# Attention and MLP gradients on one core: dw1 stored from SyncE's ring behind the last V load, and the 15-engine dV stores moved to heads 8, 17 and 26

## Chip, cores and metric

The kernel runs on one core of one Trainium2 chip. The metric is the device time of one execution in microseconds (us). The kernel before took 405.26 us when the prediction was made (median of 3 runs, 404.29 to 406.43).

Five instruction engines appear: TensorE (PE), VectorE (DVE), ScalarE (ACT), GpSimd (POOL) and SyncE (SP). The transfers are done by 16 DMA engines. "Ring" is used for the queue of transfers that one instruction engine has issued: here SyncE's ring (all large loads and some stores) and GpSimd's ring (most stores). A transfer is cut into packets, the pieces that the trace records. A semaphore is a counter that an engine can wait for; a transfer has landed when its last increment has arrived.

## The reference

One token x of width 640 passes an attention branch and an MLP branch, mixed by a gate. The reference returns the output and the gradients with respect to x, both caches and all weights.

```python
q = (x @ wq).reshape(B, Sq, H, Dh)                         # H = 32 heads, Dh = 128
scores = einsum("bhqd,bhkd->bhqk", q, k_cache) * Dh**-0.5  # 4096 keys a head
p = softmax(scores);  a = einsum("bhqk,bhkd->bhqd", p, v_cache) @ wo
act = h * tanh(softplus(h));  b = act @ w2                 # h = x @ w1 + b1, F = 1728
out = g * a + (1 - g) * b                                  # g = sigmoid(sum(x * gate_w))
return (out, *vjp(grad_out))   # dx, dk_cache, dv_cache, dwq, dwo, dw1, db1, dw2, dgate_w
```

What matters is the traffic. K and V are 1 MB for each head and each cache, read once, and dK and dV are as large and are written once. With the weights and their gradients 82.03 MB are read and 82.03 MB written. dw1 is an outer product of 640 x 1728 in bf16, 2160 KB.

## The kernel before

The main loop goes through the heads; loads are issued three heads ahead by SyncE, stores of dV and dK by GpSimd except for the last two heads. Cuts are marked.

```python
def ring(h):
    return nc.sync if h >= H - 2 else nc.gpsimd
def load_v(h):
    if h < H:
        vts[h] = kv_in.tile([P, J, Dh], BF16, name="Vn", tag="Vn", bufs=VB)
        nc.sync.dma_start(vts[h][:], Vv[h])
# ... (load_k is alike)
def dwo():                                   # gradient of wo, one group of four heads
    # ...
    (nc.sync if g == NG - 1 else nc.gpsimd).dma_start(dwo_v[g], wos[g][:])
# ...
def dw1_part(rc):
    def f():
        nc.vector.tensor_scalar(w1_sb[:, rc, :], m["dh_bc"][:], x_f[:, rc:rc + 1], None, ALU.mult)
        if rc == RC - 1:
            nc.gpsimd.dma_start(dw1_v, w1_sb[:])
    return f
# ...
def dv_half(h, half):
    # ...
    if half == 1:
        if h % 10 == 9:
            spread(h // 10, dVv[h], st["dV"])
        else:
            ring(h).dma_start(dVv[h], st["dV"][:])

def spread(i, dst, t):                       # a "15-engine store"
    # ...
    if i == 0:
        nc.gpsimd.inc_swdge_sem([], [], mode="reset_dge_cursor")
    for a, b in (((120, 125), (0, 120), (125, 128)), ((0, 14), (14, 119), (119, 128)), ((0, 8), (8, 128)))[i]:
        nc.gpsimd.dma_start(out[a:b, :], src[a:b, :], max_dma_last_dim=J * Dh)
# ...
for h in range(H):
    # ...
    load_k(h + 3)
    load_v(h + 3)
    # ...
    period(h)                                # the dK and dV halves of earlier heads are made in here
# ...
dk_half(H - 1, 0)
dk_half(H - 1, 1)
# ...
for rc in range(RC):
    nc.vector.tensor_scalar(dwq_l[:, rc, :], dq_bc[:, CL:], x_f[:, rc:rc + 1], None, ALU.mult)
nc.sync.dma_start(dwq_v[:, :, CL:], dwq_l[:])
```

An ordinary dV store sends 128 rows of 8 KB, eight to each DMA engine. `spread` cuts the same 128 rows into two or three pieces whose largest has 120 or 105 rows. It is there to give one DMA engine less to do: the largest piece goes to 15 engines and leaves one out.

## Time and profile before

| | before |
|---|---|
| time, median of 6 runs (3 more were made beside the changed kernel) | 404.82 us (404.18 to 406.43) |
| span of the profiled run | 402.6 us |
| bytes moved | 164.93 MB, mean 410 GB/s |
| PE, DVE, ACT, POOL busy | 75%, 75%, 44%, 12% |
| last DVE instruction ends | 392.62 us |
| slowest DMA engine ends its last store | 401.49 us |

From the page of the kernel before, the span, the rate in 40 slices of 10.1 us and the sum of the transfers:

```profile
span 402.6 us, 13606 instructions
...
GB/s 290 420 413 408 422 424 418 419 426 421 423 424 419 395 421 414 421 425 423 423 419 425 425 423 416 412 425 423 421 425 422 424 420 424 424 415 367 413 396 216
DMA packets 27816, 164.93 MB, mean 410 GB/s; under 512 B 3164, under 2 KB 3868, under 8 KB 11884
```

No compute engine is near full, while the rate stays at 412 to 426 GB/s in most slices. The kernel is bound by its transfers. The rate is low at the start, at slice 37 (362 to 372 us) and in the last slice. The windows view of the kernel before shows these stretches; after the bounds and the length come busy time and number of instructions of PE, PEld, DVE, ACT and POOL, the granted TensorE clock, the busy share of the 16 DMA engines, and GB/s:

```profile
core 0: us, PE busy (x) PEld busy (x) DVE busy (x) ACT busy (x) POOL busy (x), PEclk, DMA share, GB/s
357.00:362.00 5.00, 2.72 (x40) 2.38 (x37) 1.34 (x3) 1.66 (x3) 0.89 (x1) 1.00 1.01 413
362.00:367.00 5.00, 2.25 (x50) 2.02 (x50) 4.12 (x8) 1.11 (x3) 1.75 (x2) 0.78 0.89 365
367.00:372.00 5.00, 4.28 (x75) 3.92 (x75) 4.10 (x7) 2.32 (x5) 0.00 (x0) 0.88 1.02 362
387.00:392.00 5.00, 0.45 (x1) 0.18 (x1) 4.72 (x21) 0.00 (x0) 0.00 (x0) 0.50 0.93 384
392.00:397.00 5.00, 0.28 (x1) 0.09 (x1) 0.55 (x3) 0.26 (x1) 0.00 (x0) 0.50 0.91 355
397.00:403.00 6.00, 0.00 (x0) 0.00 (x0) 0.00 (x0) 0.00 (x0) 0.00 (x0) 0.50 0.27 101
```

DVE has only 1.34 us of work between 357 and 362 us. The chain of waits of the kernel before, in the window from 320 us (start, us, what), says why:

```profile
332.40 0.67 POOL out_dram L631
333.25 0.89 POOL out_dram L546
334.14 2.64 issue
336.80 25.24 DMA out_dram<-dV_sb
362.13 1.23 DVE dK_sb L614
```

L546 is the dw1 store, issued by GpSimd. Behind it in the same ring the store of dV27 took 25.24 us, and the DVE instruction that makes dK29 had to wait for that store's buffer. The timeline of DVE shows the hole as a number in brackets, 3.79 us of waiting; its last line below is DVE's last instruction:

```profile
358.17 0.17 DVE L673 TENSOR_REDUCE m<-sA 128x1 f32<-128x32 f32 x1
362.13 1.23 DVE L614 TENSOR_TENSOR dK_sb<-ds_bf,qd 128x2048 bf16<-128x2048 bf16 x1 [3.79 <-DMA out_dram<-dV_sb]
...
392.44 0.18 DVE L823 CAST fin_bf<-fin 128x15 bf16<-128x15 f32 x1
```

The waits of SyncE's queue (total us, times, longest), for its last two stores, dwo7 (L375) and dwq_l (L791):

```profile
SPq L375 <- DMA out_dram<-dV_sb: 4.9, 1, 4.9
...
SPq L791 <- DMA out_dram<-dwq_t: 1.8, 1, 1.8
```

Both wait for an earlier store to land and not for DVE. The trace's semaphore records give the reason: dwo7 and dwq_l count their completion on the semaphore of an earlier store. dV31's store is done on its slowest DMA engine at 391.35 us, and dwo7 on the same semaphore is issued at 391.42 us.

Those records also have a view that the page lacks. Each of these transfers adds 16 to its semaphore, one by one; I read every increment as one DMA engine that has done its share. They are listed here as us after the first increment, for the last half of dK31 of the kernel before (first at 390.69 us):

```
before: 0.0 0.3 0.3 0.6 1.5 1.6 3.8 4.1 5.0 5.4 5.5 5.7 7.1 7.4 7.6 7.7
```

So the DMA engines are far apart: 7.7 us between first and last, with four within 0.6 us of the last. For the last V load the spread was 16.7 us (350.17 to 366.91), one engine 5.2 us behind the next.

### The profile page before, as it was taken

The numbers are of one execution on the slowest core, as the hardware profiler recorded it, in microseconds if no ns is written. First come the engines' busy times: TensorE is split into PE (matmuls) and PEld (weight loads), VectorE is DVE, ScalarE is ACT, GpSimd is POOL, SyncE is SP. The second block draws the span as 40 slices with busy tenths as digits, with TensorE's granted clock in tenths as the row PEclk, the third lists the DMA queues.
The fourth block names the chain that finished last, engine by engine and source line by source line (L and its number), as shares of the span: only waits on it lengthen the run. The fifth ranks groups of instructions, "written<-read, shape, count | busy, mean of one in ns | idle before, by whom it ended". The sixth has DMA issues, their size and how long they took to land.

```text
span 402.6 us, 13606 instructions
## 1 busy us (share of the span) xinstructions
PE 300.7 (75%) x5872; PEld 271.9 (68%) x5872; DVE 303.7 (75%) x791; ACT 177.6 (44%) x411; POOL 46.5 (12%) x93
## 2 busy tenths in 40 slices
PE   0688888678888788878876988739887888966510
PEld 0577888568877778778866878628776778856500
DVE  3339666646599999977669799855999996968980
ACT  1355455325453555546523556505554555533300
POOL 0001111010011311111101113101111112121000
PEclk9999999857999999989988899957999999998755
DMA  8999999999999999999999999999999999999995
GB/s 290 420 413 408 422 424 418 419 426 421 423 424 419 395 421 414 421 425 423 423 419 425 425 423 416 412 425 423 421 425 422 424 420 424 424 415 367 413 396 216
DMA packets 27816, 164.93 MB, mean 410 GB/s; under 512 B 3164, under 2 KB 3868, under 8 KB 11884
## 3 DMA queue, kind: packets, MB, share of 16 engines
q1 hardware_dynamic: 16480, 91.20, 54.9%
q0 software_dynamic: 11216, 72.85, 43.7%
q8 instruction: 46, 0.75, 0.7%
q14 instruction: 14, 0.11, 0.1%
q10 hardware_dynamic: 60, 0.01, 0.0%
HBM read 82.03 MB, written 82.03 MB: 407 GB/s over the span
## 4 chain that ended last, share of the span: by engine, by line
DMA 35%; DVE 35%; PE 19%; ACT 4%; issue 3%; POOL 0%; ACTq 0%; SPq 0%; POOLq 0%; DVEq 0%
DMA Kn<-in_A_k_cache_dram 28%; DVE dK_sb L614 9%; PE tr L589 8%; DVE dV_sb L614 7%; DMA out_dram<-dV_sb 6%; DVE junk L385 4%; ACT tT L591 3%; PE sA L669 3%; DVE junk L288 3%; PE sA L598 2%; PE sB L722 2%; DVE junk L537 2%; DVE junk L494 1%; DMA vec_rows<-in_gate_w_dram 1%; DVE dj L709 1%
## 5 line engine op out<-in xcount | busy, mean ns | idle before, releaser
L591 ACT COPY tT<-tr 128x512 f32<-128x512 f32 x256 | 142.6, 588 | 138.9 <-PE tr L589 138.0
L598 PEld LDWEIGHTS <-tT 128*128 128x128 bf16 x2048 | 80.0, 98 | 43.9 <-ACT tT L591 33.8
L589 PE MATMUL tr<-ident_f,Kn 128*128 128x128 f32 x512 | 82.8, 300 | 12.8 <-DMA Kn<-in_A_k_cache_dram 12.8
L614 DVE TENSOR_TENSOR dK_sb<-ds_bf,qd 128x2048 bf16<-128x2048 bf16 x64 | 77.8, 1216 | 4.1 <-DMA out_dram<-dV_sb 3.8
L614 DVE TENSOR_TENSOR dV_sb<-p_bf,qd 128x2048 bf16<-128x2048 bf16 x64 | 78.0, 1218 | 0.6 <-DMA out_dram<-dK_sb 0.4
L589 PE MATMUL tr<-ident_f,Vn 128*128 128x128 f32 x512 | 74.3, 281 | 0.0
L589 PEld LDWEIGHTS tr<-ident_f,Kn 128*128 128x128 f32 x512 | 61.9, 153 | 14.2 <-issue 14.2
L598 PE MATMUL sA<-qd,tT 128*128 128x48 bf16 x1024 | 48.9, 187 | 23.4 <-ACT dq_all L727 12.7
L589 PEld LDWEIGHTS tr<-ident_f,Vn 128*128 128x128 f32 x512 | 57.3, 144 | 0.0
L598 PE MATMUL sB<-qd,tT 128*128 128x48 bf16 x1024 | 46.2, 183 | 0.0
L669 PEld LDWEIGHTS <-Vn 128*128 128x128 bf16 x1024 | 30.6, 96 | 10.6 <-issue 10.6
L669 PE MATMUL sA<-e_bf,Vn 128*128 128x48 bf16 x1024 | 31.2, 184 | 7.8 <-DVE zs L689 6.3
L631 POOL DMA_DIRECT2D out_dram<-dK_sb x30 | 17.2, 574 | 149.0 <-DVE rz L691 102.2
L722 PE MATMUL sB<-ds_bf,Kn 128*128 128x48 bf16 x1024 | 32.9, 187 | 1.4 <-DVE ds_bf L711 1.4
L673 DVE TENSOR_REDUCE m<-sA 128x1 f32<-128x32 f32 x32 | 6.0, 189 | 35.8 <-PE sA L598 29.1
L722 PEld LDWEIGHTS <-Kn 128*128 128x128 bf16 x1024 | 30.3, 99 | 1.6 <-issue 1.6
L644 POOL DMA_DIRECT2D out_dram<-dV_sb x27 | 14.6, 540 | 136.7 <-DVE o_all L714 48.1
L288 DVE SCALAR_TENSOR_TENSOR junk<-wo_g,da_bc 128x640 bf16<-128x640 bf16 x32 | 26.2, 820 | 1.7 <-ACT da_bc L229 1.1
L385 DVE SCALAR_TENSOR_TENSOR junk<-wq_g,dq_bc 128x1024 bf16<-128x1024 bf16 (+1 forms) x25 | 25.1, 1004 | 0.2
L693 ACT ACTIVATE p_bf<-e_bf,rz 128x64 bf16<-128x64 bf16 x32 | 11.1, 348 | 13.6 <-DVE rz L691 10.8
L700 DVE SCALAR_TENSOR_TENSOR pj<-sB,e_bf 128x32 f32<-128x32 f32 x32 | 6.1, 190 | 13.1 <-PE sB L598 12.9
L709 DVE TENSOR_SCALAR_CACHE_REDUCE dj<-sB,rz 128x128 f32<-128x128 f32 x32 | 11.1, 346 | 6.4 <-PE sB L703 6.4
(153 smaller groups left out, 275.4 us busy)
## 6 DMA issues: line engine op xcount, KB each, us to landing
Kn<-in_A_k_cache_dram SPq DMA_DIRECT2D x32, 1024.0 KB, 24.3
Vn<-in_A_v_cache_dram SPq DMA_DIRECT2D x32, 1024.0 KB, 28.8
out_dram<-dK_sb POOLq DMA_DIRECT2D x30, 1024.0 KB, 12.0
out_dram<-dV_sb POOLq DMA_DIRECT2D x27, 1024.0 KB, 11.3
wq_g<-in_A_wq_dram SPq DMA_DIRECT2D x4, 1280.0 KB, 19.7
wo_g<-in_A_wo_dram SPq DMA_DIRECT2D x8, 640.0 KB, 14.9
out_dram<-wo_g POOLq DMA_DIRECT2D x7, 640.0 KB, 11.6
out_dram<-dwq_t SPq DMA_DIRECT2D x4, 896.0 KB, 14.5
```

The lines of the kernel that those rows point to most:

```text
L288: nc.vector.scalar_tensor_tensor(junk[:, 0:D], in0=wos[g][:, i, :], scalar=1.0, in1=da_bc[:], op0=ALU.mult, op1=ALU.mult, accum_out=gp["do ...
L385: nc.vector.scalar_tensor_tensor(junk[:, c0:c1], in0=wqs[w][:, rc, c0:c1], scalar=1.0, in1=dq_bc[:, w * WG * Dh + c0:w * WG * Dh + c1], op ...
L589: nc.tensor.transpose(tp[:, t, :], flat[:, k * P:(k + 1) * P], ident_f[:])
L591: nc.scalar.copy(sb[:].rearrange("p a b -> p (a b)"), tp[:].rearrange("p a b -> p (a b)"))
L598: nc.tensor.matmul(out[:, 2 * k:2 * k + W], lhsT=tb[:, t, par, :], rhs=vec[:, par, :].unsqueeze(1).to_broadcast([P, W // 2, 2]), start=(pa ...
L614: nc.vector.tensor_tensor(dst[:, a:b, :].rearrange("p j (a b) -> p j a b", b=2), col[:, a:b, :].unsqueeze(2).to_broadcast([P, n, Dh // 2, 2]),
L631: ring(h).dma_start(dKv[h], st["dK"][:])
L644: ring(h).dma_start(dVv[h], st["dV"][:])
L669: nc.tensor.matmul(O, lhsT=vts[h][:, j, :], rhs=st["e"][:, j:j + 1].to_broadcast([P, W]), start=(j == 0), stop=(j == J - 1))
L693: nc.scalar.activation(p_bf[:], e[:].unsqueeze(2).to_broadcast([P, J, 2]), ACT.Copy, scale=rz[:])
L709: nc.vector.tensor_scalar(dj[:], PT, rz[:], None, ALU.mult, ALU.add, accum_out=dd[:])
L722: nc.tensor.matmul(DQ, lhsT=kts[h][:, j, :], rhs=ds[:, j, 0:1].to_broadcast([P, W]), start=(j == 0), stop=(j == J - 1))
```

## The change

The intent: the 2160 KB of dw1 stand in GpSimd's ring ahead of stores whose buffers DVE needs back. Put behind the last V load in SyncE's ring, where nothing follows that anybody waits for soon, dw1 delays nothing. The third 15-engine store comes at head 29 before, when the last loads have been issued; at head 26 it can still bring them forward.

```diff
             def f():
                 nc.vector.tensor_scalar(w1_sb[:, rc, :], m["dh_bc"][:], x_f[:, rc:rc + 1], None, ALU.mult)
-                if rc == RC - 1:
-                    nc.gpsimd.dma_start(dw1_v, w1_sb[:])
             return f
@@ dv_half
         if half == 1:
-            if h % 10 == 9:
-                spread(h // 10, dVv[h], st["dV"])
+            if h in (8, 17, 26):
+                spread(h // 9, dVv[h], st["dV"])
@@ main loop
+    stored = []
     for h in range(H):
         # ...
         load_k(h + 3)
         load_v(h + 3)
+        if h + 3 == H - 1 and f"dw1_{RC - 1}" in done:
+            nc.sync.dma_start(dw1_v, w1_sb[:])
+            stored.append(1)
@@ after the loop
-    assert len(dwqt) == RC
+    assert len(dwqt) == RC and stored
```

## The prediction

> **What bounds the kernel now.** The transfers. The page: 164.93 MB in 402.6 us. The windows view gives a DMA share of 1.01 to 1.02 and 413 to 425 GB/s for every 5 us from 322 to 362 us. Losses are at the start (290 GB/s in slice 1), at 362 to 372 us (365 and 362 GB/s) and in the last 6 us (share 0.27).
>
> The DMA engines are not equally far. By the sixteen completion increments of single transfers in the trace, the last K load (issued at 337.0) was done on its first engine at 345.4 and on its last at 361.8; the last V load at 350.2 and 366.9, with the slowest engine 5.2 us behind the next. At the end the spread is still 7.7 us (last dK half: 390.7 to 398.4), with four engines within 0.6 us of the last. The slow engines always have loads queued (load latency 20 to 38 us), so I read them as never idle: the kernel ends when they have moved their bytes.
>
> **What the change does.**
> 1. The dw1 store (2160 KB; at 420 GB/s 5.2 us of all engines) leaves GpSimd's ring at 333.25 us and stands in SyncE's ring behind the last V load, at about 337.9. No bytes are saved. The Trainium skill ("DMA: Bandwidth & Descriptors", Queues, rings and completion order) says that an engine goes round-robin between the rings it has work for. The trace agrees: dw1 took 23.7 us to land, and the dV and dK stores behind it 25.2, 25.6 and 23.5 us, where those before took 10 to 13. So the store of dV27 (issued 336.8) should land near 350 and not at 362.0, and the 3.79 us wait of DVE before dK29 (end of the 25.24 us link of the chain), and 0.37 us after it, go.
> 2. The third 15-engine store moves from head 29 (355 us) to head 26 (327 us), before the last loads. It spares the slowest engine 64 KB, 8 packets of about 310 ns, 2.5 us. With both, I expect the last K and V loads 3 to 6 us earlier. The other two move by one and two heads, which matters nowhere.
>
> DVE's instructions stay; their chain should end about 4 us earlier (388 to 389 instead of 392.6).
>
> **How much counts.** Little. Every engine moves the same bytes in both kernels, with three 15-engine stores either way, and those that end the kernel were busy throughout. Ending DVE's chain earlier only queues the last stores earlier: dwo7 and dwq_l already waited 4.9 and 1.8 us for earlier stores to land (waits of SyncE's queue), not for DVE. What fills is the dip at 362 to 372 us, idle time of the engines that are ahead. Against it: more of the tail is stores alone, where 8 KB packets took 315 to 336 ns. Sum: 0 to 1 us gained.
>
> **Predicted: 404.6 us, 402.4 to 406.6.** Faster by over 2%: 0.02; within: 0.96; slower: 0.02.
>
> **What would show it.** Right: no DVE wait on the dV store near 358 us; stores issued from 336 to 356 land in 10 to 15 us; the last V load lands at 361 to 364; no dip at 362 to 372; last DVE instruction near 389; and yet a spread of 6 to 9 us on the last stores, and the span within 1.5 us. Wrong: that spread falls below 5 us, or the span shrinks by the 4 us of the DVE chain.
>
> **What would make it wrong.** If the slow engines had idle time in the tail that I don't see, up to 4 us (1%) come. If the 15-engine stores relieve another engine at the new places, the end spread grows and 1 to 2 us are lost.

## The result, and the profile after

Ratios here and below are the mean time of one kernel's fast runs over that of the other's of the same rounds, so not quite the ratio of the medians that are quoted.

| | before | after |
|---|---|---|
| median of 6 runs | 404.82 us (404.18 to 406.43) | 404.14 us (403.89 to 404.53) |
| ratio to before (95% interval) | | 0.998 (0.9961 to 0.9999) |
| span of the profiled run | 402.6 us | 402.3 us |
| last DVE instruction ends | 392.62 us | 388.21 us |
| last V load done on its last engine | 366.91 us | 360.47 us |
| dV27's store, issue to landing | 25.2 us | 16.7 us |
| dw1's store, issue to landing | 23.7 us | 37.7 us |
| dwo7 and dwq_l issued | 391.42, 393.60 us | 391.31, 393.48 us |
| slowest DMA engine ends its last store | 401.49 us | 401.22 us |

All the local effects came: the DVE wait went, the loads came earlier, DVE ended 4.4 us earlier. The kernel's end moved by 0.3 us in the profiled runs.

The page of the kernel after (slice 37 is full now, slices 39 and 40 have less):

```profile
span 402.3 us, 13607 instructions
...
GB/s 283 418 416 406 419 424 420 418 422 424 422 422 418 423 414 403 425 423 423 422 421 424 423 422 419 418 426 425 421 423 425 421 424 417 425 420 417 424 368 189
```

The windows of the kernel after, same columns:

```profile
357.00:362.00 5.00, 3.72 (x68) 3.26 (x67) 4.96 (x11) 3.06 (x8) 1.14 (x2) 1.00 1.02 422
362.00:367.00 5.00, 4.47 (x104) 4.02 (x100) 4.96 (x10) 1.94 (x5) 1.50 (x2) 1.00 1.01 417
367.00:372.00 5.00, 4.28 (x92) 3.96 (x90) 4.04 (x9) 3.17 (x8) 0.00 (x0) 1.00 1.02 420
387.00:392.00 5.00, 0.27 (x1) 0.09 (x1) 1.11 (x5) 0.26 (x1) 0.00 (x0) 0.50 0.76 315
392.00:397.00 5.00, 0.00 (x0) 0.00 (x0) 0.00 (x0) 0.00 (x0) 0.00 (x0) 0.50 0.88 344
397.00:403.00 6.00, 0.00 (x0) 0.00 (x0) 0.00 (x0) 0.00 (x0) 0.00 (x0) 0.50 0.13 47
```

The dip is gone: (417 - 365) and (420 - 362) GB/s over 5 us each are 0.55 MB moved earlier. They are missing at the end: (384 - 315) + (355 - 344) over 5 us and (101 - 47) over 6 us are 0.72 MB. The bytes that filled the dip came from the share of DMA engines that would have finished early anyhow; they now idle at the end.

The timeline of DVE of the kernel after, without a bracket at dK29 and with an earlier end:

```profile
358.81 0.18 DVE L671 TENSOR_REDUCE m<-sA 128x1 f32<-128x32 f32 x1
358.91 1.22 DVE L612 TENSOR_TENSOR dK_sb<-ds_bf,qd 128x2048 bf16<-128x2048 bf16 x1
...
388.03 0.18 DVE L825 CAST fin_bf<-fin 128x15 bf16<-128x15 f32 x1
```

The waits of SyncE's queue of the kernel after:

```profile
SPq L375 <- DMA out_dram<-dV_sb: 8.9, 1, 8.9
...
SPq L793 <- DMA out_dram<-dwq_t: 1.8, 1, 1.8
```

The wait for dwo7 grew by 4.0 us, nearly all that DVE gained. Read alone, this suggests a rival reason for the small result: DVE's gain was real, and SyncE's wait for a landing swallowed it. The increments of the last half of dK31 suggest another (first at 388.50 us after, 390.69 us before):

```
before: 0.0 0.3 0.3 0.6 1.5 1.6 3.8 4.1 5.0 5.4 5.5 5.7 7.1 7.4 7.6 7.7
after:  0.0 0.3 0.3 0.5 0.6 1.3 4.1 5.4 5.6 6.3 6.8 6.9 7.0 7.1 7.2 9.6
```

In absolute time the second-last engine moved from 398.25 to 395.68 us, but the last only from 398.44 to 398.09. Before, four engines ended together; after, one stands alone, 2.4 us behind. The last increments of the last five stores come at 395.63, 396.85, 398.09, 399.64 and 401.22 us, 1.2 to 1.6 us apart for shares of 32 to 40 KB. I read them as this one engine working back to back; it ends the kernel. The recorded packets bear this out. They carry start, length and queue but no engine; yet they can be chained, as a packet mostly starts 3 or 4 ns before the end of the one before it, and the sizes must come in the order of the transfers. In the kernel after, the chain of the last engine goes back from 400.9 to 366.2 us, 201 packets with no pause over 1 ns. This is a reconstruction, which no view shows.

### The profile page after: what moved, and what is told of

Its sections match the earlier page's. It is cut to its first block, busy times and chain, and to the rows that moved or that the text cites. A ratio compares the mean times of both kernels' runs of the same rounds, so it can differ in the third digit from the quotient of the medians.

```text
span 402.3 us, 13607 instructions
## 1 busy us (share of the span) xinstructions
PE 298.5 (74%) x5872; PEld 270.1 (67%) x5872; DVE 303.1 (75%) x791; ACT 177.4 (44%) x411; POOL 45.6 (11%) x92
## 4 chain that ended last, share of the span: by engine, by line
DVE 40%; DMA 27%; PE 20%; issue 5%; ACT 4%; POOL 0%; ACTq 0%; SPq 0%; POOLq 0%
DMA Kn<-in_A_k_cache_dram 22%; DVE dK_sb L612 10%; DVE dV_sb L612 9%; PE tr L587 8%; DVE junk L385 5%; DMA out_dram<-wo_g 4%; ACT tT L589 4%; PE sA L667 3%; DVE junk L288 3%; PE sA L596 3%; PE sB L720 2%; DVE junk L537 2%; DVE junk L494 1%; DMA vec_rows<-in_gate_w_dram 1%; DVE wo_g L374 1%
## 5 line engine op out<-in xcount | busy, mean ns | idle before, releaser
L587 PE MATMUL tr<-ident_f,Kn 128*128 128x128 f32 x512 | 81.9, 298 | 12.6 <-DMA Kn<-in_A_k_cache_dram 12.6
L587 PEld LDWEIGHTS tr<-ident_f,Kn 128*128 128x128 f32 x512 | 61.2, 152 | 13.9 <-issue 13.9
## 6 DMA issues: line engine op xcount, KB each, us to landing
Kn<-in_A_k_cache_dram SPq DMA_DIRECT2D x32, 1024.0 KB, 23.7
```

The costliest lines, as they stand in the source:

```text
L587: nc.tensor.transpose(tp[:, t, :], flat[:, k * P:(k + 1) * P], ident_f[:])
```

## The experiments

The theories:

- A: the kernel ends when one DMA engine, which never idles, has moved its bytes. The change leaves that engine's bytes alone, so what DVE gains is worth nothing.
- B: DVE's chain counts, and what it gained was lost again in SyncE's waits for the semaphores of earlier stores.
- C: the bytes of all 16 engines together count.

### Each part alone

dw1 alone (against the kernel after):

```diff
-            if h in (8, 17, 26):
-                spread(h // 9, dVv[h], st["dV"])
+            if h % 10 == 9:
+                spread(h // 10, dVv[h], st["dV"])
```

> Only the dw1 store moved; the 15-engine stores stay at heads 9, 19 and 29. Theory A (the slowest DMA engine never idles and ends the kernel; its bytes are the same in before, after and here): ratio to before 0.997 to 1.001, the last transfer (dwq_l) lands within 0.6 us of 401.3, although DVE ends about 3 us earlier than in before (the wait before dK29 is gone or under 1 us; last V load lands about 363). Rival B (the tail is set by DVE's chain and the SP waits): the time follows DVE's end, -2 to -3 us.

Measured: 404.12 us (before: 405.02), ratio 0.9988 (0.9972 to 1.0004). The wait at dK29 is gone; DVE ends at 387.95 us. The last V load is hardly earlier, 366.30 us, where I had expected about 363. dV27's store took 13.8 us. The DVE timeline of this run, with no bracket:

```profile
358.63 1.21 DVE L612 TENSOR_TENSOR dK_sb<-ds_bf,qd 128x2048 bf16<-128x2048 bf16 x1
```

The moved 15-engine stores alone (against the kernel before, whose dw1 stays in GpSimd's ring):

```diff
-            if h % 10 == 9:
-                spread(h // 10, dVv[h], st["dV"])
+            if h in (8, 17, 26):
+                spread(h // 9, dVv[h], st["dV"])
```

> Only the 15-engine stores moved to heads 8, 17 and 26; dw1 stays on GpSimd. Theory A: ratio to before 0.997 to 1.002; the last K and V loads land 1.5 to 2.5 us earlier than in before (359.5, 364.7), the DVE wait before dK29 remains at 2 to 4 us, the dip in GB/s at 362 to 372 remains, dwq_l lands within 0.6 us of 401.3. Rival B: -0 to -1 us, since DVE still waits.

Measured: 404.20 us, ratio 0.9988 (0.9972 to 1.0003). The loads of K31 and V31 end at 355.05 and 359.99 us, earlier than expected. Most of DVE's wait remains, as its timeline shows:

```profile
361.67 1.23 DVE L614 TENSOR_TENSOR dK_sb<-ds_bf,qd 128x2048 bf16<-128x2048 bf16 x1 [2.95 <-DMA out_dram<-dV_sb]
```

The dip at 362 to 372 us, which I had expected to remain here, is half there: 374 and 416 GB/s by the windows view, against 407 and 417 with dw1 alone. So the wait and most of the dip belong to dw1's place, and the earlier loads to the 15-engine store at head 26. Each alone gives the same 0.1%, whether DVE's chain is shortened or not. The slowest engine's last landing is 400.96 us and 400.87 us in these two, and 401.22 us with both.

### How many 15-engine stores

None:

```diff
-            if h in (8, 17, 26):
+            if h in ():
```

> The kernel after with no 15-engine stores: all dV stores plain. Wanted: whether one engine's bytes set the time. [...]the three stores spare the slowest engine 48 + 48 + 56 KB, 19 packets of 8 KB at 0.309 us = 5.9 us. Theory A: 4 to 6 us slower than after (ratio to before 1.008 to 1.013), the last increment of the last transfers 6 to 9 us behind the second last. Rival C (the bytes of all engines together set the time): within 0.7 us of after.

Measured: 410.10 us, ratio 1.0133 (1.0117 to 1.0149): by the medians 6.0 us slower than the kernel after, as A said. The windows of this run show most engines out of work from 392 us on (the rate rises again when dwo7 is issued, at 397.82 us):

```profile
387.00:392.00 5.00, 0.45 (x1) 0.18 (x1) 4.72 (x21) 0.00 (x0) 0.00 (x0) 0.50 1.01 419
392.00:397.00 5.00, 0.28 (x1) 0.09 (x1) 0.52 (x3) 0.26 (x1) 0.00 (x0) 0.50 0.38 154
397.00:402.00 5.00, 0.00 (x0) 0.00 (x0) 0.00 (x0) 0.00 (x0) 0.00 (x0) 0.50 0.61 232
402.00:409.00 7.00, 0.00 (x0) 0.00 (x0) 0.00 (x0) 0.00 (x0) 0.00 (x0) 0.50 0.13 48
```

The increments of the last half of dK31 (first at 392.25 us):

```
none: 0.0 0.0 0.6 0.6 0.6 0.9 1.5 1.7 1.9 2.8 2.9 3.1 3.2 3.2 3.6 12.1
```

Fifteen engines are done within 3.6 us, and one is 8.5 us behind all of them. The total of bytes is the same in both kernels, which C would have equally fast: C falls.

Why three such stores spare the slow engine 6.0 us can be worked out. The Trainium skill ("DMA: Bandwidth & Descriptors", Why a DMA increments its semaphore by 16 and not by 1) says that a transfer issued by GpSimd takes the largest number of engines up to 16 that divides its rows, and that with fewer than 16 they are consecutive ones from a cursor that moves on; it names an exception for some copies, whose rows go in equal shares from engine 0 on. By the rule and not the exception, and followed through `spread` with its reset, this makes one and the same engine, number 4, the one left out by all three large pieces. The small pieces give it 2, 2 and 1 rows instead of 8, so it is spared 48, 48 and 56 KB and not 64 each: 19 packets of 8 KB, at 0.309 us (what most such packets took) an estimate of 5.9 us. By the exception engine 15 would be spared all 24 packets, an estimate of 7.4 us. No view shows engine numbers; the 6.0 us agree with the rule.

Four, and five:

```diff
-            if h in (8, 17, 26):
-                spread(h // 9, dVv[h], st["dV"])
+            if h in (5, 11, 17, 26):
+                spread({5: 0, 11: 1, 17: 0, 26: 1}[h], dVv[h], st["dV"])
```

> The kernel after with four 15-engine stores (heads 5, 11, 17 and 26). In after's trace the last increment of the last dK half comes 2.4 us after the second last (398.1 and 395.7). The pieces of these four spare the slowest engine 4 x 48 = 192 KB instead of 152 KB, 5 packets, 1.5 us. Theory A: 1 to 1.7 us faster than after (ratio to before 0.993 to 0.996), and the gap between last and second last increment falls to about 0.8 us. Rival C: within 0.3 us of after.

Measured: 402.81 us, ratio 0.9951 (0.9938 to 0.9965), 1.3 us below the kernel after by the medians. By the same count the slow engine is spared 40 KB more, five packets, an estimate of 1.5 us. The last engine is now only 0.7 us behind the second-last (396.66 and 395.95 us).

```diff
-            if h in (8, 17, 26):
-                spread(h // 9, dVv[h], st["dV"])
+            if h in (4, 9, 14, 20, 26):
+                spread({4: 0, 9: 1, 14: 2, 20: 0, 26: 1}[h], dVv[h], st["dV"])
```

> The kernel after with five 15-engine stores (heads 4, 9, 14, 20 and 26), which spare the slowest engine 48+48+56+48+48 = 248 KB, 7 packets of 8 KB = 2.2 us more than with four. In the run with four the last increment of the last dK half came only 0.6 us behind the next two, so Theory A with the next engines binding: 0 to 0.6 us faster than four (ratio to before 0.9935 to 0.9955). If one engine alone counted: 2 us faster than four (ratio 0.990).

Measured: 402.08 us (401.93 to 402.56; before in these rounds 405.11), ratio 0.9924 (0.991 to 0.9939), by the medians 0.7 us below four; the gain was a little larger than I had written. It is far less than the 56 KB more that the engine is spared would give, 7 packets or 2.2 us. The increments of dK31's last half say why (first at 387.18 us):

```
five: 0.0 0.1 0.1 0.4 0.8 3.0 5.4 6.7 8.2 8.3 8.4 8.4 8.5 8.7 8.9 9.0
```

Eight engines now end within 0.8 us of each other (the last expectation of this document counts nine). The engine that ended the kernel is no longer alone, and sparing it more would leave the others.

### Which engine is late

Four tiny loads of 4, 7, 10 and 13 rows behind the last V load, each using as many DMA engines:

```diff
         if h + 3 == H - 1 and f"dw1_{RC - 1}" in done:
+            for k in (4, 7, 10, 13):
+                pr = const.tile([16, 64], BF16, name=f"pr{k}")
+                nc.sync.dma_start(pr[0:k, :], Kv[0][0:k, 0, 0:64])
             nc.sync.dma_start(dw1_v, w1_sb[:])
```

> The kernel after with four tiny loads of 4, 7, 10 and 13 partitions in SyncE's ring right behind the last V load. By the Trainium skill a load of k such partitions on SyncE's ring runs on the lowest-numbered k engines; so each adds its own engines' completion increments right behind their share of the last V load, and tells which engines are how late. Wanted only where the late and the early ones lie. Theory A with the rule for the small pieces: the latest engine is among the lowest 7 (the 15-engine pieces leave out engine 4). If every prefix shows the same spread, the latest is engine 0 to 3; if the first prefix lacks the latest, it is another.

Measured, in one look: 404.44 us, state unknown. The Trainium skill ("DMA: Bandwidth & Descriptors", Why a DMA increments its semaphore by 16 and not by 1) says that a load issued by SyncE uses the lowest-numbered k engines and that the other 16 - k increments come at once. The trace agrees with the counts: the load of 4 rows has one early record at 339.4 us and then four increments, that of 7 rows one at 339.8 us and then seven. Their times, in us:

```
 4 rows: 351.4 351.5 351.7 353.6
 7 rows: 352.1 352.1 352.4 354.1 354.7 354.8 361.6
10 rows: 351.5 352.2 352.6 352.8 353.0 354.7 355.4 355.4 358.7 362.0
13 rows: 352.2 352.7 353.0 353.1 353.5 355.4 356.0 356.0 357.0 358.5 358.7 359.3 362.7
```

The latest appears first in the load of 7 rows, and the last V load of this run ended at 360.9 us. If the numbering is as the skill says, it is one of the engines 4, 5 and 6. That agrees with engine 4, which `spread` leaves out, but does not prove it.

### Does DVE's end count, or SyncE's wait?

DVE made late again, by four useless instructions ahead of the last group's steps (against the kernel after):

```diff
     dk_half(H - 1, 1)
+    for k in range(4):
+        nc.vector.scalar_tensor_tensor(junk[:], in0=da_bc[:, 0:1].to_broadcast([P, WG * Dh]), scalar=1.0,
+                                       in1=dq_bc[:, 0:WG * Dh], op0=ALU.mult, op1=ALU.mult)
```

> The kernel after with four DVE instructions of about 1 us, of no use, in front of the last group's steps: DVE's chain ends about 4.2 us later, as late as in before. Theory A: no change, ratio to before 0.996 to 1.000, dwo7 and dwq_l still issued near 391.3 and 393.5. If DVE's end set the time: 4 us slower, ratio 1.008.

Measured: 404.35 us (403.74 to 404.58), ratio 0.9977 (0.996 to 0.9994), as the kernel after. DVE's last instruction, by its timeline:

```profile
393.13 0.18 DVE L828 CAST fin_bf<-fin 128x15 bf16<-128x15 f32 x1
```

DVE ends at 393.31 us, 5.1 us later than after and even 0.7 us later than before, at no cost. One expectation was missed: I had dwo7 and dwq_l issued at the same times as after. The build gave them other completion semaphores, and they went out about 5 us earlier. From the timeline of SyncE's queue, first after and then this run:

```profile
391.31 0.33 SPq L375 DMA_DIRECT2D out_dram<-wo_g  x1
...
393.48 0.38 SPq L793 DMA_DIRECT2D out_dram<-dwq_l  x1
```

```profile
386.50 0.33 SPq L375 DMA_DIRECT2D out_dram<-wo_g  x1
387.82 0.38 SPq L796 DMA_DIRECT2D out_dram<-dwq_l  x1
```

Their last landing was 401.29 us all the same (401.22 after). So the miss is useful: of dwo7's 8.9 us of waiting for a landing 1.6 us were left (the waits of SyncE's queue), and nothing ended earlier.

The last two stores given to GpSimd, which has no earlier landing to wait for there, only DVE's results:

```diff
-            (nc.sync if g == NG - 1 else nc.gpsimd).dma_start(dwo_v[g], wos[g][:])
+            nc.gpsimd.dma_start(dwo_v[g], wos[g][:])
@@
-    nc.sync.dma_start(dwq_v[:, :, CL:], dwq_l[:])
+    nc.gpsimd.dma_start(dwq_v[:, :, CL:], dwq_l[:])
```

> The kernel after with the last two stores (dwo7 and dwq_l) issued by GpSimd, which need not wait until earlier stores of SyncE land (in after SyncE waits 8.9 and 1.8 us). Theory A (slowest DMA engine's bytes): issued near 381 and 383 instead of 391.3 and 393.5, but the last landing within 0.5 us of after; ratio to before 0.996 to 1.000. Rival B (the 4.4 us that DVE won were eaten by those new waits): 2 to 4 us faster than after, ratio 0.988 to 0.993.

Measured: 404.04 us (403.34 to 404.64), ratio 0.9969 (0.9952 to 0.9985); the kernel after run again beside its own rounds had 0.9976, so the difference is within the intervals. GpSimd's timeline has both stores some 11 us earlier:

```profile
380.61 0.61 POOL L375 DMA_DIRECT2D out_dram<-wo_g  x1 [18.17 <-DVE wo_g L374]
...
381.92 0.89 POOL L793 DMA_DIRECT2D out_dram<-dwq_l  x1 [0.70 <-DVE ambj L803]
```

dwq_l landed at 393.88 us, 7.3 us earlier than after, but then dK31's last half landed at 400.66 us, 2.6 us later. The last landing of all moved by 0.56 us only (0.5 at most expected). The slowest engine has the same bytes left, in another order. The Trainium skill ("DMA: Bandwidth & Descriptors", Issuing engines are not separate DMA queues) says that, whoever issues, the transfers share the same 16 engines. B, which asked for 0.988 to 0.993 here, falls.

### The kernel after, run again

Only a comment was added, for a second trace.

```diff
     return got
+# again
```

> The kernel after, unchanged, on the same chip as the two others: ratio to before 0.996 to 1.000, a second trace of it with dwq_l landing at 401.2 within 0.5 us and the last V load at 360.5 within 2 us.

Measured: 404.24 us, ratio 0.9976 (0.9959 to 0.9992). The last landing was 401.26 us, DVE's end 388.39 us, and the last engine again stood alone, 2.46 us behind the second-last (398.13 and 395.67 us). The picture is not an accident of one trace.

### Are instruction refills what makes that engine late?

The page counts 46 packets of instruction refills (queue q8, 0.75 MB, about 16 KB each). The Trainium skill ("Runtime: NRT & Kernel Launch", Instruction fetch mechanics) says that instructions are refilled in 16 KiB blocks by a DMA queue of the sequencer's own, mostly hidden. If they all fell on one DMA engine, more TensorE instructions would make that engine later. Tried with one-element matmuls to a place that nobody reads, first 24 in every head:

```diff
             s_chunk(h + 1, 1, tk)
+        for _ in range(24):
+            nc.tensor.matmul(B[0:1, 400:401], lhsT=ident_bf[0:1, 0:1], rhs=ident_bf[0:1, 0:1], start=True, stop=True)
```

> Why one engine is later than the rest. The kernel after with 24 products of one element per head into an unused PSUM word: 1536 more TensorE instructions of 64 B, 6 more refills of 16 KB (46 in before, of about 1 us each by the packets of the instruction queue), no other transfer. If the refills of TensorE's instructions all run on the engine that ends the kernel: 3.7 to 6 us slower than after, ratio to before 1.007 to 1.013, and the gap between last and second last increment of the last dK half grows from 2.4 us to 5 us or more. If they are spread over engines or run on an early one: gap unchanged, at most 1 us slower.

Measured: 408.55 us (407.27 to 410.76), ratio 1.0088 (1.0058 to 1.0119), with 52 refills. The time tells nothing about refills: transfers starved in the middle, as two windows of this run show (422 and 395 GB/s before). I take it that TensorE slowed the heads; it was hardly busier than before in the first of them (8.53 against 8.46 us), and no run tests it. The last engine was only 1.4 us behind the next, against the 5 us or more expected.

```profile
120.00:130.00 10.00, 8.53 (x208) 7.65 (x207) 9.68 (x24) 4.81 (x12) 2.46 (x4) 1.00 1.00 351
130.00:140.00 10.00, 9.49 (x233) 8.61 (x231) 9.18 (x25) 4.67 (x11) 1.14 (x2) 1.00 0.99 361
```

Then 28, in heads 13 to 23 alone:

```diff
+        for _ in range(28 if 13 <= h < 24 else 0):
+            nc.tensor.matmul(B[0:1, 400:401], lhsT=ident_bf[0:1, 0:1], rhs=ident_bf[0:1, 0:1], start=True, stop=True)
```

> The test of the refills again, without what spoiled it: in the run with more products in every head, the transfers starved at 110 to 150 us because TensorE held back the loads. Now 28 products of one element in heads 13 to 23 alone (155 to 285 us, where before TensorE has a fifth of its time free): 616 more instructions, 2 or 3 more refills. If the refills run on the engine that ends the kernel: 1.2 to 2.5 us slower than after (ratio to before 1.000 to 1.004), gap between last and second last increment of the last dK half 3.6 to 5 us where two traces of after show 2.4 and 2.5, and no dip in GB/s that was not there. If not: ratio 0.996 to 1.000 and a gap of 2 to 3 us.

Measured: 405.06 us (before in these rounds 404.82), ratio 1.0004 (0.999 to 1.0018), about 0.9 us over the kernel after. From the page of this run:

```profile
q8 instruction: 48, 0.79, 0.7%
```

Two refills more; the second-last engine ended dK31's last half at 395.94 us (395.68 after), the last at 399.28 (398.09), and the last landing was 402.40 us, 1.2 us later. The refill packets of this trace took 0.89 to 1.21 us each, so two of them on that engine would be about 2 us. The time alone would allow the refills as the cause, but the gap of 3.3 us fell short of the 3.6 to 5 expected, the rate dipped to 406 to 412 GB/s in some slices near 290 to 330 us, and it is one trace. The chained packets speak against the simple form: neither the last two refills of this trace (370.3 and 377.9 us) nor those of the kernel after (369.2 and 377.7 us) are among the last engine's packets. So not all refills run on the engine that ends the kernel. Whether enough of them do is open.

### A version that beats both

Five 15-engine stores, with the last two stores on GpSimd's ring (against the kernel after):

```diff
-            (nc.sync if g == NG - 1 else nc.gpsimd).dma_start(dwo_v[g], wos[g][:])
+            nc.gpsimd.dma_start(dwo_v[g], wos[g][:])
@@
-            if h in (8, 17, 26):
-                spread(h // 9, dVv[h], st["dV"])
+            if h in (4, 9, 14, 20, 26):
+                spread({4: 0, 9: 1, 14: 2, 20: 0, 26: 1}[h], dVv[h], st["dV"])
@@
-    nc.sync.dma_start(dwq_v[:, :, CL:], dwq_l[:])
+    nc.gpsimd.dma_start(dwq_v[:, :, CL:], dwq_l[:])
```

> Five 15-engine stores and the last two stores issued by GpSimd, on top of after: the two edits that helped, together. With five, the late nine engines ended within 0.8 us of each other, so what is left is the mean of all engines. Expected: ratio to before 0.990 to 0.993, 0 to 0.8 us faster than five alone (402.08).

Measured: 401.86 us (401.65 to 402.41; before 405.10), ratio 0.9921 (0.9904 to 0.9937), with a span of 400.0 us. It is 0.8% below the kernel before, and indistinguishable from five 15-engine stores alone (0.9924). The gain comes from the bytes of one engine, not from who issues the last stores.

## Why the prediction was right, point by point

- Time: 404.6 us predicted (402.4 to 406.6), 404.14 measured, within 2%. The argument that few of the effects lie on the critical path held, and the gain of 0 to 1 us was 0.7 us by the medians.
- The kernel ends with its slowest DMA engine, which never idles: shown for the tail, by that engine's chain of packets over the last 35 us of the kernel after; for the time before, by the runs with other numbers of 15-engine stores, as bytes spared at heads 4 to 26 came back in the time. With the same total, giving that engine more or fewer of the bytes moved the time by +6.0, -1.3 and -2.1 us; undoing DVE's 4.4 us moved nothing, and taking SyncE's waits away moved nothing beyond the intervals.
- dw1 in GpSimd's ring was what made the DVE wait: shown by dw1 alone, whose wait is gone, and by the stores alone, which keep 2.95 us of it. The prediction rested this on the skill's round-robin between rings ("DMA: Bandwidth & Descriptors", Queues, rings and completion order). The trace agrees in kind: stores that took 25.2, 25.6 and 23.5 us took 16.7, 16.4 and 15.6 us, and in the chained packets of the last engine after, packets of the two rings alternate one by one from 373 to 376 us.
- Their size was wrong. "Stores issued from 336 to 356 land in 10 to 15 us" measured 13.9 to 16.7 us, and dV27 landed at 354.24 us instead of near 350. With dw1 moved alone it took 13.8 us. No run tells what in the pair adds the difference.
- "The last V load lands at 361 to 364": it landed at 360.47 us, 6.4 us earlier instead of 3 to 6. The prediction counted 2.5 us for the 15-engine store at head 26, but the V load came 6.9 us earlier with that store alone and 0.6 us earlier with dw1 alone. The term of the store's move was the mis-sized one. What makes up the rest no run tells.
- "It spares the slowest engine 64 KB": 48 to 56 KB by the count above, as small pieces fall on it too. Three such stores would then be 24 packets or 7.4 us; taking all three away cost 6.0 us, which fits 19 packets.
- "A spread of 6 to 9 us on the last stores": 9.6 us. It grew because fifteen engines gained and one did not: the second-last ended 2.6 us earlier, the last 0.35 us. The prediction saw the risk for another reason; it missed that four tied engines would not stay tied.
- No dip at 362 to 372 us: right, 417 and 420 GB/s. With dw1 alone moved it was nearly gone (407 and 417), with the stores alone it was 374 and 416. In the trace of the kernel before, 8 KB packets of GpSimd's ring took 316 to 384 ns on average in stretches of 2 us from 364 to 372 us, with hardly any of SyncE's beside them, against about 310 ns elsewhere; that as the cause of the dip is argued, not tested.
- DVE's end: 388 to 389 us predicted, 388.21 measured.

What stays open: why that engine is later than the others. Refills are a candidate that the time of one run would allow, but that the packets of the tail do not support.

## What to carry to other kernels

When transfers bind a kernel, ask which DMA engine ends last and what bytes it alone has: the 16 increments of one late transfer show it, and the average share and rate do not. A wait that vanishes on a compute engine, or a growing wait of the issuing engine, is worth nothing if the slowest DMA engine had work queued throughout; test it by making that compute engine late again. Work taken off that one engine paid nearly in full (1.3 us of an estimated 1.5) until the next engines tied with it, here after about four 15-engine stores.

## What the Trainium skill lacked or had wrong

- No page says how far one DMA engine can fall behind in a long kernel bound by transfers, or that its bytes alone can then end the kernel. The last V load's 16 increments lay 16.7 us apart before, and without 15-engine stores one engine was 8.5 us behind all others; sparing it bytes was worth 6.0 us.
- "DMA: Bandwidth & Descriptors", Latency and other measured facts, calls engines 7 and 15 usually slower. Here the latest was, by that page's own numbering rule, one of engines 4 to 6, counted from 0: absent from the load on the first four, present from the load on the first seven on (361.6 us against 354.8 for the next).
- "Runtime: NRT & Kernel Launch", Instruction fetch mechanics, calls the refills mostly hidden and does not say how much time of a DMA engine one takes. Here each was one packet of 16 KB that took 0.88 to 1.14 us, 46 in the trace of the kernel before (0.75 MB). Two more went with a last landing 1.2 us later, in one run; that they were the cause is not shown.
- "DMA: Bandwidth & Descriptors", Why a DMA increments its semaphore by 16 and not by 1, warns of two transfers in flight on one semaphore. It does not say that a build that keeps them apart makes the issuing engine wait: 8.9 us for dwo7 after, issued 0.06 us after dV31's store on the same semaphore landed (391.25 us). It cost nothing here.
